# One core: the first pair's q and k on two queues by units, one mask made ahead of the branch, and the bias of the first block scaled in pieces

## The chip, the cores and the metric

The kernel runs on one core of a Trainium2 chip. The metric is the device time of one execution in microseconds (us); the kernel before has a median of 492.08 us over three runs (492.0 to 493.21).

## What is computed

The program is a banded attention, followed by two mixing layers. Cut to what matters here:

```python
scores = scale * np.matmul(q, k.transpose(0, 1, 3, 2))      # 2 batches, 8 heads, 768 rows, 64 wide
rel = pos[:, None] - pos[None, :]
is_global = pos[None, :] < int(n_global)
is_local = (rel >= 0) & (rel < int(n_local))
keep = is_global | is_local
dist = np.where(is_global & ~is_local, float(n_local), np.abs(rel))
scores = np.where(keep, scores + -slopes * dist, -1e9)
a = np.exp(scores - max); a = a / (sum + 1e-9); attn = a @ v
# then, on x = the heads side by side (2 x 768 x 512):
u = x + (relu(x.T @ w_tok1) @ w_tok2).T;  x = u + relu(u @ w_ch1) @ w_ch2
theta = x @ w_theta;  y = w_tok_r @ (x * cos(theta)) + w_tok_i @ (x * sin(theta))
u = x + y;  out = u + relu(u @ w_ch)
```

`n_global` (8) and `n_local` (96) are inputs. The program reads them at run time and branches: where they fit a band it takes the fast path (`attention_band`), else a dense one.

## The kernel before, in words

The whole kernel is written in program order (`manual_schedule`), so each engine runs its instructions in the order in which the code issues them. Around the change the order is this, with the lines of the kernel before.

**Ahead of the branch** (`run`, L895 on). SyncE (SP) issues the DMA of the two counts (`load_counts`, L237), then those of the first pair's k and q in two pieces each, k first (`load_first`, L351 and L352), and later the first pair's v and its shifted copy `a` (L367 to L370). VectorE (DVE) clears a piece of `x[1]` that serves as zeros (L907). TensorE (PE) runs ten matmuls on zeros (`warm_up`, L330). ScalarE (ACT) loads its function table and computes one exponential (L230). GpSimd (POOL) makes the identity and three integer ramps (`ramps`, L267), and ACT turns them into floats (L269). Then every engine loads the counts into registers with two TENSOR_LOADs (L913), evaluates the condition and branches (L918).

**Behind the branch** `band_bias` (L275 on) builds `base`, three 128-column blocks that are the same for all heads: `base0` (columns 0 to 128) for the first row block of each head, and `base1` (columns 128 to 384) for all others, made of `before` (96 columns), `seen` (32 columns) and `own` (128 columns). POOL makes the mask `past` (L286), the far term and `seen` (L292, L295); DVE makes the counts as floats (L290), `own` (L302, L305), `before` (L302, L305) and the first 32 columns of `base0` as a maximum of `own` and `seen` (L310); ACT copies the other 96 columns of `base0` (L308). Then each head gets a copy of all 384 columns times its slope: ACT for heads 0 and 1 (L317), POOL for heads 2 to 7 (L319).

**`attention_band`** goes through 24 units, each two row blocks of a pair of heads; a pair has three units. In step u it issues the scores of unit u (PE, L437), their bias and row minimum (DVE, L450), the exponentials (ACT, L574 and L578), the transposes of unit u-1 (PE, L484; copied back on ACT or DVE, L494 and L496) and the values of unit u-2 (PE, L406), finished on DVE and POOL (L390 to L382). Loads for the next pairs are issued inside this loop. In step 1, POOL clears two strips of the next pair's v and `a` tiles (`tiles_v`, L360), SP issues their DMAs (`load_v`, L367 to L370, which wait for those strips), then a weight job (L125), then q and k of the pair after that (L338, L339). So q and k of the third pair, which unit 6 reads first, stand in SP's queue behind v and `a` of the second pair, and these behind POOL's strips, and the strips behind POOL's six scalings of L319.

After the attention come the token mix, the channel mix and the last layer; the change does not touch them.

```python
            for u in range(N + 2):
...
                if u < N and oi + 1 < len(order) and ip == 1:
                    nx = order[oi + 1]
                    self.tiles_v(pairs_pool, pairs[nx], *nx)
                    self.load_v(pairs[nx], *nx)
                    if oi == 0:
                        self.prefetch(1)
                    if oi + 2 < len(order):
                        pairs[order[oi + 2]] = self.load_qk(pairs_pool, *order[oi + 2], bufs=2)
```

Of the kernel before, what the change touches and what calls it, by code (L numbers as in the profile page):

```python
# [15 lines left out]
F32 = mybir.dt.float32  # L16
# [3 lines left out]
AF = mybir.ActivationFunctionType  # L20
ALU = mybir.AluOpType
# [3 lines left out]
B, H, S, D = 2, 8, 768, 64  # L25
P = 128
NS = S // P
# [8 lines left out]
NG = 32  # L36
# [4 lines left out]
SCALE = 0.125  # L41
BIG = 2.56e11
# [14 lines left out]
def slope(h):  # L57
    return 2.0 ** (-(h + 1.0))
# [25 lines left out]
class Build:  # L84
# [177 lines left out]
    def ramps(self, pool):  # L262

        self.ramp = []
        for n, base, mult in ((P, 0, -1), (PREV, -PREV, -1), (NG, 0, 0)):
            ti = pool.tile([P, n], I32, name="ramp_i%d" % n)
            self.nc.gpsimd.iota(ti, pattern=[[1, n]], base=base, channel_multiplier=mult)  # L267
            tf = pool.tile([P, n], F32, name="ramp%d" % n)
            self.nc.scalar.copy(out=tf, in_=ti)  # L269
            self.ramp.append(tf)  # L270

    def band_bias(self, pool):

        nc = self.nc
        ng, nl = self.nvf[:, 0:1], self.nvf[:, 2:3]
        base = pool.tile([P, 3 * P], F32, name="base")  # L280
        base0, base1 = base[:, 0:P], base[:, P : 3 * P]
        before, seen, own = base1[:, 0:PREV], base1[:, PREV:P], base1[:, P : 2 * P]
        with self.tc.tile_pool(name="bb", bufs=1) as tp:
            d_own, d_prev, gcol = self.ramp
            past = tp.tile([P, P], F32, name="past")
            nc.gpsimd.affine_select(  # L286
                out=past, in_=d_own, pattern=[[-1, P]], compare_op=ALU.is_ge, fill=-BIG,
                base=0, channel_multiplier=1,
            )
            nc.vector.tensor_copy(out=self.nvf, in_=self.nvi)  # L290
            g = tp.tile([P, NG], F32, name="far_g")
            nc.gpsimd.tensor_scalar(  # L292
                out=g, in0=gcol, scalar1=ng, scalar2=-BIG, op0=ALU.is_ge, op1=ALU.mult
            )
            nc.gpsimd.tensor_scalar(out=seen, in0=g, scalar1=nl, scalar2=None, op0=ALU.subtract)  # L295
            nnl = tp.tile([P, 1], F32, name="nnl")
            nc.vector.tensor_scalar(out=nnl, in0=nl, scalar1=-1.0, scalar2=None, op0=ALU.mult)

            def near(out, t, dist, tag):

                far = tp.tile([P, t.shape[1]], F32, name="far" + tag)
                nc.vector.tensor_scalar(  # L302
                    out=far, in0=dist, scalar1=nnl, scalar2=-BIG, op0=ALU.is_le, op1=ALU.mult
                )
                nc.vector.tensor_tensor(out=out, in0=far, in1=t, op=ALU.add)  # L305

            near(own, past, d_own, "own")
            nc.scalar.copy(out=base0[:, NG:P], in_=own[:, NG:P])  # L308
            near(before, d_prev, d_prev, "prev")
            nc.vector.tensor_tensor(  # L310
                out=base0[:, 0:NG], in0=own[:, 0:NG], in1=seen, op=ALU.max
            )
        self.base = []
        for h in range(H):
            t = pool.tile([P, 3 * P], F32, name="base%d" % h)
            if h < 2:
                nc.scalar.activation(out=t, in_=base, func=AF.Copy, scale=slope(h) / SCALE)  # L317
            else:
                nc.gpsimd.tensor_scalar(  # L319
                    out=t, in0=base, scalar1=slope(h) / SCALE, scalar2=None, op0=ALU.mult  # L320
                )
            self.base.append((t[:, 0:P], t[:, P : 3 * P]))

# [16 lines left out]
    def load_first(self, pool):  # L342

        t = dict(
            q=pool.tile([P, S], F32, name="q_0_0", tag="q"),
            k=pool.tile([P, NS, KW], F32, name="k_0_0", tag="k"),
        )
        q, k = self.dram["q"][0, 0], self.dram["k"][0, 0]
        for i0, i1 in ((0, 2), (2, NS)):
            qs = slice(i0 * P, i1 * P)  # L350
            self.nc.sync.dma_start(out=t["k"][:, i0:i1], in_=k[:, i0:i1])  # L351
            self.nc.sync.dma_start(out=t["q"][:, qs], in_=q[:, qs])  # L352
        return t

# [1018 lines left out]
```

## Time and profile before

| | |
|---|---|
| median of three runs | 492.08 us (492.0 to 493.21) |
| the profiled execution | 493.28 us, of which the span of the core's instructions is 491.5 us |
| granted TensorE clock over the span | 1.0 of full speed |
| PE busy | 484.3 us (99%), 2836 matmuls |
| DVE, ACT, POOL busy | 317.4 us (65%), 262.9 us (53%), 180.8 us (37%) |
| chain that ended last, by engine | PE 83%, DVE 5%, ACT 5%, POOL 3%, DMA 2%, issue 1% |
| DMA | 50.66 MB, mean 103 GB/s |

The busy shares say which engine has the most work. What sets the end is read from the chain: it is followed back from the last instruction, at each step to whatever released it. The span leaves out 1.78 us of the execution's time, which lie around the instructions. In the rows below a time in the first column is counted from the span's start; "SPq", "DVEq" and the like are the sequencers that hand instructions to their engines and issue DMAs.

### The profile page before, as it was taken

Reading aid. Unit: us, or ns where it says so; the run is one execution under the profiler, and the core shown is the slowest. Engines: PE = TensorE matmul, PEld = TensorE weight load, DVE = VectorE, ACT = ScalarE, POOL = GpSimd, SP = SyncE. Lnnn points to the kernel's source line nnn. Section 1 sums busy time; section 2 is a strip of 40 time slices with the busy share of each in tenths; the row PEclk is TensorE's granted clock in tenths of the full one; section 3 lists DMA queues with packets and bytes.
Section 4 is the critical chain, followed back from the end, with each engine's and each line's share of the span. In section 5 each row is a group of like instructions: output and inputs, shape, how many; then the busy total and the mean of one; then the engine's idle time right before and its main releaser. Section 6 shows DMA issues by size and latency. Waiting matters only on the chain.

```text
span 491.5 us, 7645 instructions
## 1 busy us (share of the span) xinstructions
PE 484.3 (99%) x2836; PEld 412.3 (84%) x2836; DVE 317.4 (65%) x671; ACT 262.9 (53%) x482; POOL 180.8 (37%) x187
## 2 busy tenths in 40 slices
PE   8999999999999999999999999999999999999997
PEld 4788888787888888888888888888888889988896
DVE  4688787854776689506656564687998866351442
ACT  6888777723565554204569464646776566322010
POOL 7345534430443575401323241334554633333000
PEclk9999999999999999999999999999999999999999
DMA  6687863401454545302444222524210101000012
GB/s 194 202 261 219 280 209 119 129 2 50 134 172 107 158 137 143 94 1 85 147 133 149 87 56 60 141 87 104 68 23 22 44 22 23 21 23 22 23 71 101
DMA packets 49022, 50.66 MB, mean 103 GB/s; under 512 B 20944, under 2 KB 39888, under 8 KB 48976
## 3 DMA queue, kind: packets, MB, share of 16 engines
q1 hardware_dynamic: 48976, 50.08, 34.6%
q8 instruction: 25, 0.41, 0.3%
q14 instruction: 21, 0.17, 0.1%
HBM read 42.21 MB, written 3.15 MB: 92 GB/s over the span
## 4 chain that ended last, share of the span: by engine, by line
PE 83%; DVE 5%; ACT 5%; POOL 3%; DMA 2%; issue 1%; DVEq 0%; SPq 0%; POOLq 0%; ACTq 0%
PE gp L96 20%; PE h L96 18%; PE y L96 13%; PE v L96 7%; PE mm L96 7%; PE o L406 5%; PE th L96 5%; PE t L484 4%; PE s L437 4%; DMA k<-k 2%; POOL base L319 1%; ACT cut_xt L789 1%; DVE x L1061 1%; DVE w L1154 1%; POOL s L1180 1%
## 5 line engine op out<-in xcount | busy, mean ns | idle before, releaser
L149 POOL TENSOR_TENSOR cvt<-cvt,cvs 128x512 int32<-128x512 int32 (+1 forms) x57 | 75.1, 1318 | 177.2 <-DVE cvt L148 144.0
L96 PE MATMUL h<-wc,g 128*128 128x512 f32 x432 | 101.7, 389 | 0.0
L96 PE MATMUL gp<-xh,wc 128*128 128x512 f32 (+1 forms) x384 | 97.1, 335 | 0.0
L96 PEld LDWEIGHTS h<-wc,g 128*128 128x128 f32 x432 | 79.6, 188 | 15.2
L96 PEld LDWEIGHTS gp<-xh,wc 128*128 128x128 f32 x384 | 67.2, 189 | 8.6 <-DVE g L708 0.2
L708 DVE SCALAR_TENSOR_TENSOR g<-gp,g 128x512 fp32r<-128x512 f32 (+1 forms) x48 | 26.7, 556 | 63.4 <-ACT g L706 63.1
L96 PE MATMUL gp<-xl,wc 128*128 128x512 f32 (+1 forms) x192 | 64.3, 335 | 0.0
L96 PE MATMUL y<-wri,s 128*128 128x256 f32 (+1 forms) x288 | 52.0, 335 | 0.2 <-POOL s L1180 0.2
L96 PE MATMUL y<-wri,z 128*128 128x256 f32 (+1 forms) x288 | 51.9, 335 | 0.0
L706 ACT ACTIVATE g<-gp 128x512 fp32r<-128x512 f32 (+1 forms) x48 | 23.4, 486 | 53.2 <-PE gp L96 53.2
L96 PEld LDWEIGHTS y<-wri,s 128*128 128x128 f32 x288 | 44.7, 189 | 6.4 <-POOL s L1180 0.4
L96 PEld LDWEIGHTS y<-wri,z 128*128 128x128 f32 x288 | 44.6, 188 | 5.9
L484 PE MATMUL t<-ident,e 128*128 128x128 f32 x176 | 48.1, 285 | 0.4 <-ACT at L496 0.4
L145 DVE SCALAR_TENSOR_TENSOR cvs<-cvt,cvs 128x512 int32<-128x512 int32 (+1 forms) x57 | 44.8, 787 | 0.1
L96 PEld LDWEIGHTS gp<-xl,wc 128*128 128x128 f32 x192 | 36.0, 188 | 4.7
L450 DVE CUSTOM_DVE_ANT_0 e<-s,base 128x256 f32<-128x256 f32 (+1 forms) x96 | 32.9, 397 | 9.1 <-PE s L437 7.1
L484 PEld LDWEIGHTS t<-ident,e 128*128 128x128 f32 x176 | 31.7, 184 | 8.1 <-issue 2.3
L139 ACT ACTIVATE cvt<-raw 128x512 f32<-128x512 f32 (+1 forms) x57 | 37.2, 653 | 2.2 <-issue 2.2
L140 ACT ACTIVATE cvs<-raw 128x512 int32<-128x512 uint16 (+1 forms) x57 | 37.4, 656 | 0.0
L96 PE MATMUL th<-s,xt 128*128 128x512 f32 x144 | 34.9, 391 | 0.0
L1157 ACT ACTIVATE w<-w 128x512 f32<-128x512 f32 x12 | 7.6, 632 | 49.4 <-DVE w L1154 49.4
L406 PE MATMUL o<-v,at 128*128 128x65 f32 x192 | 32.3, 252 | 0.0
(111 smaller groups left out, 839.9 us busy)
## 6 DMA issues: line engine op xcount, KB each, us to landing
raw<-w_ch SPq DMA_DIRECT2D x28, 512.0 KB, 4.1
raw<-w_tok SPq DMA_DIRECT2D x21, 512.0 KB, 4.2
k<-k SPq DMA_DIRECT2D x7, 480.0 KB, 5.6
v<-v SPq DMA_DIRECT2D x8, 384.0 KB, 3.7
out<-o SPq DMA_DIRECT2D x11, 256.0 KB, 2.0
q<-q SPq DMA_DIRECT2D x7, 384.0 KB, 4.7
raw<-w_theta SPq DMA_DIRECT2D x4, 512.0 KB, 4.0
a<-v SPq DMA_DIRECT2D x8, 240.0 KB, 4.5
```

Source lines behind the costliest of these rows:

```text
L96: self.nc.tensor.matmul(out, lhsT=a, rhs=b, start=first and i == 0, stop=last and i == n - 1)
L139: nc.scalar.activation(out=f(t), in_=f(top), func=AF.Copy, scale=2.0**-111)
L140: nc.scalar.activation(out=s, in_=nxt, func=AF.Copy, scale=2.0**-13)
L145: nc.vector.scalar_tensor_tensor(out=s, in0=t, scalar=-(1 << 31), in1=s, op0=ALU.bitwise_and, op1=ALU.bitwise_or)
L149: nc.gpsimd.tensor_tensor(out=t, in0=t, in1=s, op=ALU.add)
L406: self.nc.tensor.matmul(po[:, j * OW : j * OW + D + 1], lhsT=at, rhs=v[:, j * (D + 1) : (j + 1) * (D + 1)], start=first, stop=last,)
L437: nc.tensor.matmul(ps[j][:, ii, c0:], lhsT=t["q"][pj, i * P : (i + 1) * P], rhs=kf[pj, i * KW - P + c0 : i * KW + P], start=True, stop=True,)
L450: nc.vector.tensor_tensor_reduce(out=e, in0=ps[j][:, ii, c0:], in1=self.base[2 * hp + j][min(i, 1)], op0=ALU.add, op1=ALU.min, scale=-SCAL ...
L484: nc.tensor.transpose(pt[:, ii, c, :], e[j][:, ii, c * P : (c + 1) * P], self.ident)
L706: nc.scalar.activation(out=hi, in_=ps, func=AF.Relu if relu else AF.Copy)
L708: nc.vector.scalar_tensor_tensor(out=lo, in0=ps, scalar=0.0, in1=f(hi), op0=ALU.max, op1=ALU.subtract)
L1157: nc.scalar.activation(out=a, in_=t, func=AF.Abs)
```

## The change

Three edits, in the first microseconds of the program.

1. `load_first`: q and k of the first pair come in three pieces each (two row blocks to a piece) rather than two. The pieces of k are issued on ACT's queue, those of q on SP's.
2. `ramps`: the floats are made by DVE rather than ACT, and POOL makes `past` right there, ahead of the branch, in a free piece of `x[1]`.
3. `band_bias`: `base0`'s first 32 columns are made ahead of `before`. ACT scales the pieces of the first block for heads 0 and 1 (96 and 32 columns each), then their 256 columns of `base1`, and copies the 96 columns into `base0` last. POOL's six scalings follow as before.

```diff
@@ -266,8 +266,13 @@
             ti = pool.tile([P, n], I32, name="ramp_i%d" % n)
             self.nc.gpsimd.iota(ti, pattern=[[1, n]], base=base, channel_multiplier=mult)
             tf = pool.tile([P, n], F32, name="ramp%d" % n)
-            self.nc.scalar.copy(out=tf, in_=ti)
+            self.nc.vector.tensor_copy(out=tf, in_=ti)
             self.ramp.append(tf)
+        self.past = self.x[1][:, 1, 0:P]
+        self.nc.gpsimd.affine_select(
+            out=self.past, in_=self.ramp[0], pattern=[[-1, P]], compare_op=ALU.is_ge, fill=-BIG,
+            base=0, channel_multiplier=1,
+        )
 
     def band_bias(self, pool):
 
@@ -282,11 +287,6 @@
         before, seen, own = base1[:, 0:PREV], base1[:, PREV:P], base1[:, P : 2 * P]
         with self.tc.tile_pool(name="bb", bufs=1) as tp:
             d_own, d_prev, gcol = self.ramp
-            past = tp.tile([P, P], F32, name="past")
-            nc.gpsimd.affine_select(
-                out=past, in_=d_own, pattern=[[-1, P]], compare_op=ALU.is_ge, fill=-BIG,
-                base=0, channel_multiplier=1,
-            )
             nc.vector.tensor_copy(out=self.nvf, in_=self.nvi)
             g = tp.tile([P, NG], F32, name="far_g")
             nc.gpsimd.tensor_scalar(
@@ -304,22 +304,29 @@
                 )
                 nc.vector.tensor_tensor(out=out, in0=far, in1=t, op=ALU.add)
 
-            near(own, past, d_own, "own")
-            nc.scalar.copy(out=base0[:, NG:P], in_=own[:, NG:P])
-            near(before, d_prev, d_prev, "prev")
+            near(own, self.past, d_own, "own")
             nc.vector.tensor_tensor(
                 out=base0[:, 0:NG], in0=own[:, 0:NG], in1=seen, op=ALU.max
             )
-        self.base = []
-        for h in range(H):
-            t = pool.tile([P, 3 * P], F32, name="base%d" % h)
-            if h < 2:
-                nc.scalar.activation(out=t, in_=base, func=AF.Copy, scale=slope(h) / SCALE)
-            else:
-                nc.gpsimd.tensor_scalar(
-                    out=t, in0=base, scalar1=slope(h) / SCALE, scalar2=None, op0=ALU.mult
-                )
-            self.base.append((t[:, 0:P], t[:, P : 3 * P]))
+            near(before, d_prev, d_prev, "prev")
+        ts = [pool.tile([P, 3 * P], F32, name="base%d" % h) for h in range(H)]
+
+        def scaled(h, src, c0, c1):
+            nc.scalar.activation(
+                out=ts[h][:, c0:c1], in_=src, func=AF.Copy, scale=slope(h) / SCALE
+            )
+
+        for h in range(2):
+            scaled(h, own[:, NG:P], NG, P)
+            scaled(h, base0[:, 0:NG], 0, NG)
+        for h in range(2):
+            scaled(h, base1, P, 3 * P)
+        nc.scalar.copy(out=base0[:, NG:P], in_=own[:, NG:P])
+        for h in range(2, H):
+            nc.gpsimd.tensor_scalar(
+                out=ts[h], in0=base, scalar1=slope(h) / SCALE, scalar2=None, op0=ALU.mult
+            )
+        self.base = [(t[:, 0:P], t[:, P : 3 * P]) for t in ts]
 
 
 
@@ -346,9 +353,9 @@
             k=pool.tile([P, NS, KW], F32, name="k_0_0", tag="k"),
         )
         q, k = self.dram["q"][0, 0], self.dram["k"][0, 0]
-        for i0, i1 in ((0, 2), (2, NS)):
-            qs = slice(i0 * P, i1 * P)
-            self.nc.sync.dma_start(out=t["k"][:, i0:i1], in_=k[:, i0:i1])
+        for i0 in range(0, NS, 2):
+            qs = slice(i0 * P, (i0 + 2) * P)
+            self.nc.scalar.dma_start(out=t["k"][:, i0 : i0 + 2], in_=k[:, i0 : i0 + 2])
             self.nc.sync.dma_start(out=t["q"][:, qs], in_=q[:, qs])
         return t
```

**ACT ahead of the branch.** `one` is the exponential of L230, the TENSOR_LOADs fetch the counts. Before:

```order
L230 ACT_TABLE_LOAD
L230 ACTIVATE one<-halfpi 128x1 [waits DVE_49]
L269 CAST ramp_130<-ramp_i_128 128x128 [waits Pool_49]
L269 CAST ramp_134<-ramp_i_132 128x96 [waits Pool_49]
L269 CAST ramp_138<-ramp_i_136 128x32 [waits Pool_49]
L913 TENSOR_LOAD nv_ptr
L913 TENSOR_LOAD nv
```

and with the change:

```order
L358 DMA k_0_102<-k 128x320 x3
L230 ACT_TABLE_LOAD
L230 ACTIVATE one<-halfpi 128x1 [waits DVE_49]
L920 TENSOR_LOAD nv_ptr
L920 TENSOR_LOAD nv
```

Three DMA issues stand ahead of the table load now, and the three conversions are gone.

**DVE ahead of the branch.** `x_66` are the zeros, a wait on Pool is one for POOL's ramps. Before:

```order
L907 MEMSET x_66 128x256
L228 MEMSET halfpi 128x1
L913 TENSOR_LOAD nv_ptr
L913 TENSOR_LOAD nv
L918 ISA
```

and with the change:

```order
L914 MEMSET x_66 128x256
L228 MEMSET halfpi 128x1
L269 CAST ramp_132<-ramp_i_130 128x128 [waits Pool_49]
L269 CAST ramp_136<-ramp_i_134 128x96 [waits Pool_49]
L269 CAST ramp_140<-ramp_i_138 128x32 [waits Pool_49]
L920 TENSOR_LOAD nv_ptr
L920 TENSOR_LOAD nv
L925 ISA
```

Three instructions that wait for POOL stand ahead of DVE's two loads now.

**ACT and POOL behind the branch.** `base_303` and the tile numbered next to it are the scaled copies of heads 0 and 1, those that POOL writes belong to heads 2 to 7. ACT before:

```order
L308 COPY base<-base 128x96 [waits DVE_49]
L317 ACTIVATE base_303<-base 128x384 [waits DVE_49,Activation_49]
L317 ACTIVATE base_305<-base 128x384
L574 ACTIVATE e_0_330<-e_0_330,mn_329 128x128 [waits DVE_49]
L574 ACTIVATE e_0_331<-e_0_331,mn_329 128x128 [waits DVE_49]
```

and with the change:

```order
L315 ACTIVATE base_303<-base 128x96 [waits DVE_49]
L315 ACTIVATE base_303<-base 128x32 [waits DVE_49]
L315 ACTIVATE base_304<-base 128x96
L315 ACTIVATE base_304<-base 128x32
L315 ACTIVATE base_303<-base 128x256 [waits DVE_49,Pool_49]
L315 ACTIVATE base_304<-base 128x256
L324 COPY base<-base 128x96
L581 ACTIVATE e_0_335<-e_0_335,mn_334 128x128 [waits DVE_49]
```

POOL before:

```order
L286 AFFINE_SELECT past<-ramp_130 128x128 [waits Activation_49]
L292 TENSOR_SCALAR far_g<-ramp_138,nvf 128x32 [waits DVE_49,Activation_49]
L295 TENSOR_SCALAR base<-far_g,nvf 128x32 [waits Pool_49]
L319 TENSOR_SCALAR base_307<-base 128x384 [waits DVE_49,Activation_49]
L319 TENSOR_SCALAR base_309<-base 128x384
```

and with the change:

```order
L292 TENSOR_SCALAR far_g<-ramp_140,nvf 128x32 [waits DVE_49]
L295 TENSOR_SCALAR base<-far_g,nvf 128x32 [waits Pool_49]
L326 TENSOR_SCALAR base_305<-base 128x384 [waits DVE_49,Activation_49,Pool_49]
L326 TENSOR_SCALAR base_306<-base 128x384
L326 TENSOR_SCALAR base_307<-base 128x384
```

ACT's copy into `base` went from the first to the last place of its bias work: two whole scalings stood behind it, six by pieces stand ahead of it. POOL's first scaling waits for that copy (Activation) as it did before; in both kernels four more scalings follow the rows shown, and then the two strips of the second pair's v and `a` (L360, now L367).

## Rows read from the trace of the kernel before

**Rows 1.** The page's first line.
```profile
span 491.5 us, 7645 instructions
```

**Rows 2.** Who PE waited for, whole span: us in total, times, longest us.
```profile
PE s L437 <- DMA q<-q: 0.8, 1, 0.8
PE s L437 <- DMA k<-k: 0.7, 1, 0.7
```

**Rows 3.** The chain that ended last, 0 to 30 us: start us, us, what.
```profile
5.99 4.59 POOL base L319 x4
...
15.81 7.91 DMA k<-k
...
23.86 0.93 PE s L437 x8
```

**Rows 4.** Instructions behind the branch: start us, us, engine, line, op, out<-in.
```profile
4.03 0.17 DVE L290 CAST nvf<-nvi 128x4 f32<-128x4 int32 x1 [2.89 <-DMA nvi<-nv]
...
4.56 0.50 POOL L292 TENSOR_SCALAR far_g<-ramp,nvf 128x32 f32<-128x32 f32 x1
4.89 0.29 DVE L305 TENSOR_TENSOR base<-farown,past 128x128 f32<-128x128 f32 x1
...
5.15 0.45 POOL L295 TENSOR_SCALAR base<-far_g,nvf 128x32 f32<-128x32 f32 x1
5.28 0.27 ACT L308 COPY base<-base 128x96 f32<-128x96 f32 x1 [2.56 <-DVE base L305]
5.39 0.26 DVE L305 TENSOR_TENSOR base<-farprev,ramp 128x96 f32<-128x96 f32 x1
5.63 0.19 DVE L310 TENSOR_TENSOR base<-base 128x32 f32<-128x32 f32 x1
...
5.92 0.94 ACT L317 ACTIVATE base<-base 128x384 f32<-128x384 f32 x2 [0.37 <-DVE base L310]
5.99 7.08 POOL L319 TENSOR_SCALAR base<-base 128x384 f32<-128x384 f32 x6 [0.39 <-DVE base L310]
...
6.80 0.81 ACT L574 ACTIVATE e<-e,mn 128x128 f32<-128x128 f32 x2
```

**Rows 5.** Instructions and DMA issues ahead of the branch, in order of time.
```profile
0.73 1.28 ACT L230 ACT_TABLE_LOAD   x1 [0.73 <-PEq L1352]
...
1.19 0.42 SPq L351 DMA_DIRECT2D k<-k  x1
...
1.26 0.50 POOL L267 IOTA ramp_i<- 128x128 int32 x3
...
1.66 0.42 SPq L352 DMA_DIRECT2D q<-q  x1
...
2.14 0.57 ACT L269 CAST ramp<-ramp_i 128x128 f32<-128x128 int32 x3
```

**Rows 6.** Register loads (L913), ACT's branch (L918): ns min/median/max, first, last start us.
```profile
L913 DVEq TENSOR_LOAD <-nv_ptr x1: 911/911/911, 0.8 to 0.8; - x1
...
L913 PEldq TENSOR_LOAD <-nv_ptr x1: 932/932/932, 1.2 to 1.2; - x1
...
L913 ACTq TENSOR_LOAD <-nv_ptr x1: 1017/1017/1017, 2.0 to 2.0; - x1
...
L913 SPq TENSOR_LOAD <-nv_ptr x1: 2880/2880/2880, 4.7 to 4.7; - x1
...
L918 ACTq COMPARE_BRANCH x2: 38/42/45, 4.7 to 115.7; - x2
```

**Rows 7.** k of the third and fourth pair: KB, us from issue to landing.
```profile
k<-k SPq DMA_DIRECT2D x1, 480.0 KB, 7.9
...
k<-k SPq DMA_DIRECT2D x1, 480.0 KB, 5.8
```

**Rows 8.** Two stretches: us, PE, PEld, DVE, ACT, POOL busy, PE clock, DMA share, GB/s.
```profile
23.16:23.86 0.70, 0.01 (x1) 0.04 (x2) 0.63 (x4) 0.70 (x3) 0.00 (x0) 1.00 0.19 60
23.86:33.74 9.88, 9.88 (x92) 8.49 (x92) 7.33 (x34) 8.10 (x20) 4.73 (x9) 1.00 0.83 267
```

## The prediction

> **What bounds the kernel now.** I read the views from the end backwards. Whole-span waits first: PE waits for data twice among its longest waits, 0.8 us for q and 0.7 us for k [rows 2], in a span of 491.5 us [rows 1]. So whatever moves the end must move PE, and the change touches only the first microseconds. The chain says which of the two waits counts. It runs from the bias work into POOL's scalings from 5.99, through SP's queue to a DMA of k issued at 15.81 that takes 7.91 us, and into PE's scores at 23.86 [rows 3]; these belong to unit 6, the first of the third pair. From there on PE is its link almost throughout: in the 9.88 us behind it PE is busy for 9.88 [rows 8]. The wait for k, 23.16 to 23.86, is therefore the place where the first part of the program sets the end. The wait for q lies ahead of it and is swallowed by it: PE, earlier by 0.8 us, would wait 0.8 us longer for k.
>
> Why is k late? It is issued behind the second pair's v, which waits for POOL's strips, and these for six scalings of 1.18 us (7.08 in all) that start at 5.99 [rows 4]. **The end hangs on when POOL starts scaling**, with no slack: PE already waits. POOL starts 0.17 us after DVE's maximum ends (5.63 + 0.19 = 5.82) [rows 4].
>
> **DVE's three conversions.** An instruction that waits for another engine holds back the register loads behind it: PE's load starts at 1.2, with its ten warm matmuls still to run, where DVE, with nothing to wait for, starts at 0.8 [rows 6]. Now three conversions stand ahead of DVE's loads, and wait for POOL's ramps, of which the third ends at 1.26 + 0.50 = 1.76 [rows 5]. DVE's loads so start at 1.8 rather than 0.8. From there to the float counts at 4.03 took 3.2 us [rows 4]; they come at 5.0. The conversions themselves (0.57 us for three on ACT [rows 5]) lie beside the loads.
>
> **`past` moved.** It leaves the branch, and far_g, which started at 4.56 behind it [rows 4], now waits for the counts, which end at 5.0 + 0.17: it starts at 5.2, and from its start to the end of `seen` is 5.15 + 0.45 - 4.56 = 1.04 us [rows 4], so 6.27. Ahead of the branch `past` waits for DVE's first conversion, and POOL's loads come some 0.7 us later; DVE's being later still hides that.
>
> **The bias on DVE.** `own` ends 4.89 + 0.29 - 4.03 = 1.15 us behind the counts' start [rows 4]: 6.15. The maximum, now ahead of `before`, needs `seen`: 6.3 to 6.5. The last step of `before` starts 0.50 behind the preceding add (4.89 to 5.39) and lasts 0.26 [rows 4]: 6.8 to 7.06. The chain that ended at 5.82 ends at 7.06.
>
> **ACT.** Three DMA issues at SP's pitch of 0.47 (1.19 to 1.66) [rows 5] push the table load from 0.73 to 2.15, by 1.4 us; the three conversions that leave ACT gave nothing, since its loads started at 2.0, as the table load ended, ahead of their execution [rows 5, 6]. ACT's first load started at 2.0 and its branch at 4.7 [rows 6]; moved by 1.4 us ACT is free at some 6.15. No row shows a DMA issue on ACT; its bounds are nothing and twice SP's 0.47 each (two sequencers at once), and I take SP's, the same instruction. Then seven operations: four pieces of 96 and 32 columns at a pitch of 0.19 (three conversions in 0.57 [rows 5]), the first at about 6.25 with `own`, the second at 6.6 with the maximum, the fourth at 7.0; the two of 256 columns with `before` at 7.16. Their pitch lies between 0.19 and the 0.42 of 384 columns (0.94 for two, 0.52 for one [rows 4]); I take 0.32, by its width nearer to the latter. The copy starts at 7.8 and takes 0.27 as at 5.28 [rows 4]: 8.07. The Trainium skill ("ScalarE: Activation LUTs", What ACT_TABLE_LOAD costs) prices a 256-column piece at 186 + 0.833 x 256 = 399 ns and takes off 93 ns of overlap, so 0.31; by it the sum would be the same within 0.02 us.
>
> **The sum.** POOL starts 0.17 behind the copy, at 8.24 in place of 5.99: **2.2 us later**, and so do the strips, v, `a`, the weight job, q and k. Six scalings and the transfers are unchanged. k's landing moves from 23.72 to 25.9 and unit 6's scores to 26.1. The exponentials of unit 0 start behind the copy, at 8.1 rather than 6.80 [rows 4]; ACT had idle time then, so half a microsecond of that reaches PE. It is covered by the wait for k, which has 2.2 us more, and would cost 0.5 us if k were not late. The split of q and k saves up to 0.8 us in unit 1, covered by the same wait. So the profiled execution of 493.28 us would become 495.5; that execution lies 1.2 us above the median of 492.08, and from the median I forecast **494.3 us**. Bounds of this case: with pitch 0.19 and the counts at 4.8, +1.7; with 0.42 and DMA issues longer by half on ACT (ACT then decides, at 6.9), +2.9: 493.8 to 495.0.
>
> **Rivals.**
> - *ACT's loads are held behind its DMA issues.* SP's first load, right behind its DMA issues, took 2.88 us, where ACT's took 1.02 [rows 6]. If ACT, now an issuer too, meets the same, it is free at 8.0; four pieces (0.76), two of 256 (0.64), the copy and the start (0.44) put POOL at 9.85: +3.9, 496.0 us. For it: the same kind of queue. Against it: ACT has 1.28 us of table load between its issues and its load, and SP's last issues were those of v and `a`, not of k. The Trainium skill ("DMA: Bandwidth & Descriptors", Queues, rings and completion order) says that SP and ACT have rings of their own on the same 16 DMA engines but no descriptor generator of their own; by it ACT could stand behind SP's v and `a` as well. No run here shows ACT as an issuer. Chance 0.16.
> - *The holding does not happen.* If DVE's loads ran ahead of the waiting conversions, the counts would come at 4.03, `seen` at 5.3, `before` at 6.1, and the copy would end at 7.1 with ACT free in time: POOL at 7.3, +1.3, 493.4 us. Rows 6 speak against it. Chance 0.10.
> - *Not slower: k's transfer gives the time back.* k took 7.9 us from its issue, the next pair's k 5.8 [rows 7]. Landing 2.1 us sooner behind its issue it would be where it was, 23.7, and the time 492.1 us; it decides from 1.5 us saved (a landing within 6.4 us). The 60 GB/s at 23.16 to 23.86 [rows 8] say that the transfer then ran at its tail, on few of the DMA engines. Against it: the five transfers ahead of it, and their order, stay. Chance 0.10.
> - *The clock falls.* PE would stand idle for up to 2.9 us rather than 0.7 ahead of unit 6. The granted clock stayed at 1.00 through the 0.7 us wait [rows 8]. If it fell to its lower level (1.2 GHz, half of 2.4), one unit's work, 9.88 / 3 = 3.3 us [rows 8], would take twice as long: 494.3 + 3.3 = 497.6 us. The Trainium skill ("TensorE: Matmul & The Clock Gate", What's actually happening) says that the clock follows how busy the PE has been; no stretch of this trace shows a fall. Chance 0.04.
>
> **How the numbers follow.** The first case has 0.60. The range leaves out the clock, half of the case in which k gives the time back, and a small part of ACT's loads being held longer: 492.4 to 496.3 us. About 0.3%, 1.5 us, is what a measurement of this kernel can tell from no change (the three runs lie 1.2 us apart). Slower by more: most of the first case, ACT's loads and the clock, 0.73. Within: the holding that does not happen, most of k's case, and the lowest end of the first, 0.22. Faster by more would need more than both of PE's waits gone, 0.8 + 0.7 us [rows 2]; 0.05 for what I do not see.
>
> **What would show it.** Right: DVE's loads start near 1.8, the counts near 5.0, ACT's table load near 2.15, POOL's first scaling near 8.2, k of the third pair is issued near 18, and PE waits two to three us for it or for the v and `a` ahead of it in the queue; the 0.8 us wait for q is gone. Wrong: POOL's first scaling below 7.5, or at 8.2 with PE waiting under 1.5 us; a load on ACT of over 2 us would mean the first rival.

## The result: slower by 1.0%, about twice the forecast

The changed kernel took 497.49 us (median of five runs, 495.9 to 500.22) against 492.98 for the kernel before (five runs): a ratio of 1.0102 over all runs (the two medians alone give 1.0091), 95% interval 1.0085 to 1.0118. The direction was as forecast. The size was not: 4.5 us instead of 2.2, and the median lies above the range, which ended at 496.3.

The profile after is of the run of 500.22 us. Its page opens with these rows:

```profile
span 498.4 us, 7652 instructions
...
PEclk9959999999999999999999999999999999999999
```

The span is 6.9 us longer than that of before [rows 1], and in the third of forty slices the granted TensorE clock fell to half. The five runs had mean clocks of 0.989, 0.997, 0.999, 0.992 and 0.996, and their times mostly follow: 500.22, 497.49, 495.9, 498.36, 496.75.

The chain still runs through the float counts, POOL's scalings, SP's queue and k of the third pair. The same instructions in the changed kernel, from the timeline (start us, us, engine, line):

```profile
6.32 0.17 DVE L290 CAST nvf<-nvi 128x4 f32<-128x4 int32 x1 [4.06 <-issue]
...
9.51 7.09 POOL L326 TENSOR_SCALAR base<-base 128x384 f32<-128x384 f32 x6 [1.83 <-DVE mn L457]
...
19.33 0.43 SPq L346 DMA_DIRECT2D k<-k  x1
...
26.64 1.65 PE L444 MATMUL s<-k,q 64*128 64x128 f32 x8 [1.99 <-DMA k<-k]
```

The counts come at 6.32 instead of 4.03 and POOL starts at 9.51 instead of 5.99 [rows 4]. PE waits 1.99 us for k, and the scores of unit 6 start at 26.64 instead of 23.86 [rows 3]. They also take 1.65 us instead of 0.93. The stretches table says why (us, PE, PEld, DVE, ACT, POOL busy, PE clock, DMA share, GB/s):

```profile
24.65:26.64 1.99, 0.00 (x2) 0.03 (x1) 0.60 (x2) 1.37 (x3) 1.13 (x2) 0.93 0.94 315
26.64:36.56 9.92, 9.92 (x50) 8.32 (x51) 4.47 (x21) 3.86 (x9) 2.40 (x3) 0.50 0.73 235
36.56:41.09 4.53, 4.53 (x44) 3.92 (x42) 2.71 (x12) 3.36 (x9) 1.23 (x4) 1.00 0.00 0
```

For 9.92 us behind the wait PE worked at half its clock: 50 matmuls, where 9.88 us of before held 92 [rows 8]. Unit 9's scores start 14.38 us behind unit 6's (26.64 to 41.02) instead of 9.81 (23.86 to 33.67). So the profiled run lost 2.8 us up to unit 6 and 4.6 us to the clock behind it, and got back some 0.5 later.

Why the counts are so late stands in the register loads (line 920; ns min/median/max, first and last start us):

```profile
L920 PEldq TENSOR_LOAD <-nv_ptr x1: 1013/1013/1013, 1.2 to 1.2; - x1
...
L920 DVEq TENSOR_LOAD <-nv_ptr x1: 1531/1531/1531, 1.9 to 1.9; - x1
L920 ACTq TENSOR_LOAD <-nv_ptr x1: 1669/1669/1669, 2.2 to 2.2; - x1
L920 PEldq TENSOR_LOAD <-nv x1: 2774/2774/2774, 2.3 to 2.3; - x1
...
L920 DVEq TENSOR_LOAD <-nv x1: 1961/1961/1961, 3.4 to 3.4; - x1
```

In the kernel before the second loads of DVE and PE were these:

```profile
L913 DVEq TENSOR_LOAD <-nv x1: 1346/1346/1346, 1.8 to 1.8; - x1
...
L913 PEldq TENSOR_LOAD <-nv x1: 1084/1084/1084, 2.2 to 2.2; - x1
```

DVE's first load starts at 1.9, close to the forecast 1.8, and then both its loads are long: 1.53 and 1.96 us, where they took 0.91 [rows 6] and 1.35 before. PE's second load starts when it did before, within 0.1 us, and takes 2.77 us instead of 1.08; that engine's program did not change, so something around it did. The DMAs of that time are late too (KB, us from issue to landing; k's first piece and the counts):

```profile
k<-k ACTq DMA_DIRECT2D x1, 160.0 KB, 4.0
nvi<-nv SPq DMA_DIRECT2D x1, 2.0 KB, 3.8
```

In the kernel before each of the two needed 2.8 us:

```profile
k<-k SPq DMA_DIRECT2D x1, 160.0 KB, 2.8
...
nvi<-nv SPq DMA_DIRECT2D x1, 2.0 KB, 2.8
```

### The profile page after: what moved, and what is told of

The parts are those of the page before. It is cut to its first block, busy times and chain, and to the rows that moved or that the text cites. A ratio compares the mean times of both kernels' runs of the same rounds, so it can differ in the third digit from the quotient of the medians.

```text
span 498.4 us, 7652 instructions
## 1 busy us (share of the span) xinstructions
PE 490.2 (98%) x2836; PEld 416.1 (83%) x2836; DVE 318.4 (64%) x674; ACT 262.8 (53%) x483; POOL 180.7 (36%) x187
## 4 chain that ended last, share of the span: by engine, by line
PE 83%; DVE 5%; ACT 5%; POOL 3%; DMA 1%; issue 1%; DVEq 1%; SPq 0%; POOLq 0%; ACTq 0%
PE gp L96 20%; PE h L96 18%; PE y L96 13%; PE v L96 7%; PE mm L96 7%; PE o L413 6%; PE th L96 4%; PE t L491 4%; PE s L444 4%; DMA k<-k 1%; POOL base L326 1%; ACT cut_xt L796 1%; DVE x L1068 1%; DVE w L1161 1%; DVEq L920 1%
## 5 line engine op out<-in xcount | busy, mean ns | idle before, releaser
L491 PE MATMUL t<-ident,e 128*128 128x128 f32 x176 | 50.0, 295 | 0.8 <-ACT at L503 0.4
L491 PEld LDWEIGHTS t<-ident,e 128*128 128x128 f32 x176 | 33.0, 192 | 9.8 <-issue 4.2
```

Source lines behind the costliest of these rows:

```text
L491: nc.tensor.transpose(pt[:, ii, c, :], e[j][:, ii, c * P : (c + 1) * P], self.ident)
```

## The experiments

Two theories were on record when the first four ran: that two queues which issue at once slow the start, loads and transfers alike, and that the loads crowd each other because edit 2 moves them together. The second question was whether the clock falls because PE idles.

**Edit 1 alone, on the kernel before.**

```diff
-        for i0, i1 in ((0, 2), (2, NS)):
-            self.nc.sync.dma_start(out=t["k"][:, i0:i1], in_=k[:, i0:i1])
+        for i0 in range(0, NS, 2):
+            self.nc.scalar.dma_start(out=t["k"][:, i0 : i0 + 2], in_=k[:, i0 : i0 + 2])
```

> The kernel before with edit 1 alone (k on ACT's queue, three pieces each). Theory 'two queues': two queues that issue at once slow the first microseconds for transfers and for the register loads alike. It expects DVE's two loads to take 1.5 + 2.0 us as in the changed kernel instead of 0.9 + 1.35, the counts at 5.2 instead of 4.03 us, POOL's first scaling at about 7.2 instead of 5.99, PE's wait for k at 1.5 to 2 us, and the time 1.2 us above before. Rival 'crowding': the loads are slow because edit 2 moves DVE's and POOL's loads together with ACT's. It expects DVE's loads at 0.9 + 1.35 here, POOL at 5.99 within 0.2, and the time of before within 0.4 us.

494.09 us against 492.85: 1.0032 (1.0019 to 1.0046). Its loads and POOL's start:

```profile
L913 DVEq TENSOR_LOAD <-nv x1: 2365/2365/2365, 1.8 to 1.8; - x1
...
L913 PEldq TENSOR_LOAD <-nv x1: 2401/2401/2401, 2.6 to 2.6; - x1
```

```profile
7.65 7.08 POOL L319 TENSOR_SCALAR base<-base 128x384 f32<-128x384 f32 x6 [0.39 <-DVE base L310]
```

Without edits 2 and 3 the loads are about as long as in the changed kernel: DVE's two take 0.92 + 2.37 = 3.29 us, against 1.53 + 1.96 = 3.49 there and 2.26 before. The counts come at 5.06 and PE waits 1.6 us for k. Crowding by edit 2 falls. The clock fell in the profiled run here as well, and not at once (from the wait's start at 23.59 us):

```profile
23.59:25.19 1.60, 0.00 (x1) 0.03 (x1) 0.79 (x4) 1.60 (x4) 0.57 (x2) 1.00 0.69 222
25.19:30.06 4.87, 4.87 (x32) 4.47 (x32) 2.24 (x10) 2.29 (x7) 1.83 (x2) 0.65 1.03 280
```

In the first microsecond behind the wait the clock was still 0.96; from 26.2 us on it was 0.50.

**Edits 2 and 3 alone: k and q back on SP in two pieces.**

```diff
-        for i0 in range(0, NS, 2):
-            self.nc.scalar.dma_start(out=t["k"][:, i0 : i0 + 2], in_=k[:, i0 : i0 + 2])
+        for i0, i1 in ((0, 2), (2, NS)):
+            self.nc.sync.dma_start(out=t["k"][:, i0:i1], in_=k[:, i0:i1])
```

> The changed kernel with edit 1 undone (k and q on SP's queue, two pieces each). Theory 'two queues' expects the register loads at their old length (DVE 0.9 + 1.35), the counts at 5.0, POOL's first scaling at 8.0 to 8.3, k of the third pair 2 to 2.3 us later than before, and 2.2 us above before, plus what the clock loses if it falls in the wait. Rival 'crowding' expects DVE's loads at 1.5 + 2.0, the counts at 6.3, POOL at 9.5 and the time of the changed kernel, some 4.5 us above before.

494.92 us, 1.0043 (1.0026 to 1.006), at clocks from 0.993 to 1.0. From its timeline and its register loads:

```profile
5.18 0.17 DVE L290 CAST nvf<-nvi 128x4 f32<-128x4 int32 x1 [2.92 <-issue]
...
8.38 7.08 POOL L326 TENSOR_SCALAR base<-base 128x384 f32<-128x384 f32 x6 [1.83 <-DVE mn L457]
```

```profile
L920 DVEq TENSOR_LOAD <-nv_ptr x1: 1500/1500/1500, 1.9 to 1.9; - x1
...
L920 DVEq TENSOR_LOAD <-nv x1: 852/852/852, 3.4 to 3.4; - x1
```

This is nearly the sum of the prediction: counts at 5.0, POOL at 8.24, 2.2 us (2.1 measured). DVE's first load took 1.50 us here and its second 0.85, 2.35 together, near the 2.26 of before. Two of its five runs lost clock all the same (498.08 us at 0.993, the profiled one, and 495.58 at 0.996), so the 2.1 us are those of the median.

**All six pieces on SP's queue.**

```diff
-            self.nc.scalar.dma_start(out=t["k"][:, i0 : i0 + 2], in_=k[:, i0 : i0 + 2])
+            self.nc.sync.dma_start(out=t["k"][:, i0 : i0 + 2], in_=k[:, i0 : i0 + 2])
```

> The changed kernel with all six pieces on SP's queue (k ahead of q). If two queues slow the start, this one is as fast as the run with edit 1 undone: the counts at 5.0, POOL at 8.0 to 8.3, 2 to 3 us above before. If the smaller pieces do it, the counts stay at 6.3, POOL at 9.5, 4.5 us above before. ACT's table load starts at 0.73 in either case.

495.07 us, 1.0061 (1.0035 to 1.0087); the counts at 4.79, POOL at 7.99. The smaller pieces are not at fault, the use of the second queue is. (With it the six transfers are also issued sooner, the last at about 2.1 us instead of 3.55; the runs do not separate the two.) Its profiled run of 494.55 us also had PE wait 1.92 us, as long as the changed kernel's, and kept its clock:

```profile
23.40:25.32 1.92, 0.01 (x1) 0.03 (x1) 0.80 (x4) 1.81 (x4) 0.88 (x2) 1.00 0.79 245
25.32:35.20 9.88, 9.88 (x92) 8.50 (x92) 7.17 (x33) 6.98 (x17) 3.84 (x8) 1.00 0.72 231
```

Others of its runs did not: 0.990 at 499.42 us, 0.996 at 496.48 and 496.36, 0.997 at 495.24.

**PE's wait filled with matmuls on zeros.**

```diff
+                    if u == 6:
+                        self.warm_up(6)
                     exps = scores(u)
```

> The changed kernel with six matmuls on zeros put ahead of the scores of unit 6, where PE waits 2.0 us for k; nothing else moves. Theory 'clock': the clock falls because PE idles there, and that costs the runs between 0.5 and 4.5 us. It expects a granted clock of 1.00 in every stretch, PE's scores of unit 6 still at 26.6 us and all runs within 1 us of 495.8 us, the changed kernel's run at a clock of 0.999. Rival 'the wait alone': the clock has another cause; it expects the clock at 0.99 to 0.997 again and a median of 497.5 us.

`warm_up(6)` issues six matmuls on zeros. 495.83 us (495.45 to 497.08, four runs), clocks of 1.0 three times and 0.999. The stretches:

```profile
24.65:26.43 1.78, 0.96 (x4) 0.26 (x4) 0.49 (x2) 1.49 (x3) 1.08 (x2) 1.00 0.86 282
26.43:36.31 9.88, 9.88 (x92) 8.50 (x92) 7.17 (x33) 6.98 (x17) 3.65 (x8) 1.00 0.77 239
```

POOL is as late (9.62), k nearly as late, PE still waits for it (0.82 us behind the zeros), and the clock stays. That takes 1.7 us off the changed kernel's median, with no other change. One run of four (497.08) lies outside the expected 1 us, without a fall of the clock that would explain it.

**The copy first again**, on the run with edit 1 undone.

```diff
             near(own, self.past, d_own, "own")
+            nc.scalar.copy(out=base0[:, NG:P], in_=own[:, NG:P])
...
-        nc.scalar.copy(out=base0[:, NG:P], in_=own[:, NG:P])
```

> The run with edit 1 undone, and ACT's copy of 96 columns put back into the first place of its bias work. If the copy's last place costs POOL what the sum says (ACT's six scalings ahead of it, about 1.0 us), POOL's first scaling starts at about 7.3 instead of 8.4 and the time falls to 1.0 to 1.3 us above before, mostly at a clock of 1.00. If POOL is late only by the counts, it stays at 8.2 or later and 2 us above before.

```profile
5.46 0.17 DVE L290 CAST nvf<-nvi 128x4 f32<-128x4 int32 x1 [3.29 <-issue]
...
7.72 7.09 POOL L326 TENSOR_SCALAR base<-base 128x384 f32<-128x384 f32 x6 [0.89 <-ACT base L316]
```

From the counts to POOL's start it is 2.26 us here, 3.20 in the run with edit 1 undone and 3.19 in the changed kernel: the copy's last place costs 0.94. The counts came 0.3 later than in the run with edit 1 undone, so POOL gained only 0.66. Nothing ahead of the counts differs between these two programs, so 0.3 us is what the loads vary by, with one queue (PE's second took 1.62 us here and 1.03 there). In time this is a miss: 494.64 us, 1.0046 (1.0022 to 1.0071), not clearly below the 494.92, and 2.1 us above the before measured beside it, as there. Its eight runs go from 493.27 to 498.85, the slowest at a clock of 0.988; three of them lie at 493.3 to 493.6, about where the expectation put it.

**The strips ahead of the scalings**, in both kernels. `rest` holds POOL's scalings of heads 2 to 7, which leave `band_bias`.

```diff
             pairs[order[1]] = self.load_qk(pairs_pool, *order[1], bufs=2)
+            self.tiles_v(pairs_pool, pairs[order[1]], *order[1])
+            self.rest()
             for u in range(N + 2):
...
-                    self.tiles_v(pairs_pool, pairs[nx], *nx)
+                    if oi:
+                        self.tiles_v(pairs_pool, pairs[nx], *nx)
```

The changed kernel with this move:

> The changed kernel with the two strips of the second pair's v and a made by POOL ahead of its six scalings, so that the DMAs of v, a, the weight job, q and k no longer wait for these. If the whole loss runs through that queue (k's landing, and the clock that falls in the wait for it), PE does not wait for k at unit 6, the clock stays at 1.00 and the time is that of before within 1 us (492 to 494), though the register loads are as slow as in the changed kernel. If the slow start costs PE something of its own (its first scores came 1.2 us later, the exponentials of unit 0 2.5 us later), that shows now: 494 to 495.

493.43 us, 1.0018 (1.0009 to 1.0027), ten runs from 493.19 to 493.86, all at 0.999 or 1.0. Counts at 6.47 and POOL at 9.67, later than ever, and yet PE waits for no k:

```profile
PE s L447 <- issue: 0.5, 1, 0.5
PE t L494 <- ACT e L586: 0.4, 1, 0.4
PE t L494 <- ACT e L590: 0.3, 1, 0.3
```

So most of the loss came through that one queue, by k's landing and by the clock behind it: 4.1 us between the two medians, 3.6 when each is counted against the before measured beside it. The rest, 0.9 us, is PE's own later start: the scores of units 0 and 2 start at 6.12 and 11.34 us here, and at 5.26 and 9.71 in the kernel before with the same move, the next run.

The kernel before with the move, and with q and k in six pieces on SP besides:

> The kernel before with the same move of the two strips. The sum expects PE's wait of 0.7 us for k gone and 0.5 to 0.8 us less time than before, 492.1 against 492.85. If k still lands late for another reason (the first pairs' transfers crowd each other when they start sooner), the wait stays and so does the time.

> The same, and the first pair's q and k in six pieces on SP's queue. PE's wait of 0.8 us for q at unit 1 should go too, and now nothing behind it swallows it: 0.3 to 0.8 us less than the run with the strips alone. If ACT's exponentials bound units 0 to 2 anyway, the time is that of the run with the strips alone, within 0.3 us.

Both missed: 492.52 us, 0.9999 (0.999 to 1.0008), and 492.43 us, 0.9999 (0.999 to 1.0008). The wait for k is gone in both profiles, and the time is that of before. Two more traces of the kernel before were taken to see what the gain had been counted against.

> The kernel before, unchanged, for a second trace of it. In nine traces so far the time from unit 6's first score to the end of the span, at a clock of 0.999 to 1.00, is 467.2 to 467.7 us. So a run at before's median of 492.6 (span 490.8) should have unit 6's scores at 23.2 to 23.6 and a wait for k of 0 to 0.5 us instead of 0.7: that would be why moving the strips gains nothing. If the wait is 0.7 or more at a time of 492.6, the gain went somewhere else.

> The same once more: unit 6's scores at the span minus 467.2 to 467.7 us, and the wait for k longer the longer the span.

492.3 and 492.71 us. The first has its unit 6 here, and neither trace has a wait for k at all:

```profile
23.09 0.93 PE L437 MATMUL s<-k,q 64*128 64x128 f32 x8
```

```profile
k<-k SPq DMA_DIRECT2D x1, 480.0 KB, 6.8
```

In the second unit 6 starts at 23.34, and k landed 7.2 us behind its issue. The 0.7 us of the profile that the prediction read [rows 2] belong to a run of 493.28 us in which k took 7.9 [rows 7]; in the other two it landed 0.4 to 0.5 us ahead of unit 6. The issue of that DMA alone took 1.55 us in the first profile, and 0.43 in each of the other two, which may be why (the second row is of the first further trace):

```profile
15.81 1.55 SPq L339 DMA_DIRECT2D k<-k  x1
```

```profile
15.76 0.43 SPq L339 DMA_DIRECT2D k<-k  x1
```

In all ten traces with a mean clock of 0.999 or 1.0 from unit 6's first score to the end of the span it is 467.1 to 467.7 us. The start of unit 6 and the clock behind it are all that the first part of the program passes on.

**When do two queues hurt?** The last two put k's three issues on ACT behind its table load (`load_first_k`), and only k's first piece on ACT.

```diff
                     self.constants(cp)
+                    self.load_first_k(first)
```

> The changed kernel with k's three issues on ACT behind its table load, so from about 2.1 us instead of 0.74. What slows the first microseconds could be two queues that start at the same moment (0.74 to 2.1 us), or any time in which both issue. The first expects the counts at 5.0 to 5.3 and POOL at 8.2 to 8.5; the second the counts at 6 or later again. Either way k of unit 0 lands later than in the changed kernel if a transfer needs as long as there (4.0 us from its issue): PE's first scores at about 6.2 or later.

```diff
-            self.nc.scalar.dma_start(out=t["k"][:, i0 : i0 + 2], in_=k[:, i0 : i0 + 2])
+            eng = self.nc.scalar if i0 == 0 else self.nc.sync
+            eng.dma_start(out=t["k"][:, i0 : i0 + 2], in_=k[:, i0 : i0 + 2])
```

> The changed kernel with k's first piece alone on ACT's queue, the other five pieces on SP's. If a second queue in use is enough to slow the start, the first transfers take 3.8 to 4.0 us again and the counts come at 6.0 to 6.4. If it is the number of transfers in two queues at once, the counts come at 4.8 to 5.3 as with one queue. ACT's table load moves by 0.47 us only, to 1.2.

Behind the table load: 497.64 us, 1.0102 (1.0085 to 1.0118), the counts at 6.72. With one piece: 493.99 us, 1.0049 (1.0024 to 1.0074), the counts at 4.73, POOL at 7.92, as with one queue; k's piece on ACT landed after 3.3 us. So a second queue in use is not enough: with three transfers on each the start is slow, with one on ACT it is not. Two on ACT were not tried. From the timeline of the run behind the table load:

```profile
0.73 1.28 ACT L230 ACT_TABLE_LOAD   x1 [0.73 <-PEq L1364]
1.20 0.87 ACTq L364 DMA_DIRECT2D k<-k  x2
...
2.10 0.45 ACTq L364 DMA_DIRECT2D k<-k  x1
```

The first two issues start at 1.20, in the middle of the table load, so "behind" it is 0.46 us later than in the changed kernel and not 1.4, and the moment of the start was put to the test more weakly than meant: a shift of 0.46 us changes nothing, a longer one was not tried. Its PE scores of unit 0 came at 5.57, not at 6.2 or later. The counts' own transfer landed after 2.9 us here, almost as before, and the counts came later than in any other run: it is the register loads that hold them (DVE's took 1.87 and 2.03 us). ACT's first load, right behind its last issue, took 3.06 us. What in the chip makes loads and transfers slow then was not found.

## Why the prediction was wrong

**Right.** The bound (POOL's start, through SP's queue, to k of the third pair), the direction, the holding of DVE's loads behind its conversions (1.8 forecast, 1.9 measured), the 3.2 us from the counts to POOL's start (8.24 - 5.0; measured 3.19), and that the wait for q goes without a gain. Of the signs that the prediction named, ACT's table load at 2.15 and PE's wait of two us (1.99) are there; k is issued at 19.33, not near 18. With edit 1 undone the sum holds as it stands: POOL at 8.38, 2.1 us. That the time agrees so closely is partly luck, since the sum had no slack and two traces of before have 0.4 to 0.5 us.

**The first step that failed: "From there to the float counts at 4.03 took 3.2 us; they come at 5.0".** It kept the length of DVE's loads. They took 3.49 us instead of 2.26, and the counts came at 6.32. This is a term of 1.3 us, and edit 1 brings it: DVE's two loads take 3.29 us with edit 1 alone, and 2.35 with edits 2 and 3 alone. The prediction had a rival for slow loads and tied it to ACT alone, as a follower of its own DMA issues, because SP's load behind such issues was the only long one in the rows [rows 6]. ACT's first load did take 1.67 us (it started at 2.2, straight behind the issues: the table load that was held against this rival lay beside it, not between), but PE's and POOL's, which issue no DMA, grew as well, and DVE's decided. That the rival's start for POOL, 9.85, lies near the measured 9.51 is luck. The page cited there ("DMA: Bandwidth & Descriptors" of the Trainium skill) says in its section Issuing engines are not separate DMA queues that issuing from several engines only saves the time of the issue. The saving is there: SP issues v at 2.60 us, with all six pieces on SP at 4.03. The runs add a price that the page does not have: with k's three pieces on ACT, its first landed 4.0 us behind its issue instead of 2.8, the counts 3.8 instead of 2.8.

**The second: the clock, at a chance of 0.04.** "The granted clock stayed at 1.00 through the 0.7 us wait" was true, and it was taken as evidence for a wait of up to four times that length, 2.9 us, of which no row spoke. In the changed kernel four runs of five had a mean clock below 0.999; the profiled run gave up 4.6 us, the rival had priced 3.3. That its 497.6 us lies so near the median is luck: by the estimate below the median run lost more ahead of unit 6 and less to the clock than the rival has it. This step puts the median outside the range: without the fall, in the filled wait, it is 495.83 us, which lies inside. The filled wait shows the cause: PE's idling. The rule of the Trainium skill ("TensorE: Matmul & The Clock Gate", What's actually happening), that the clock follows how busy PE has been, agrees: 0.50 for 9.92 us behind the wait, 1.00 with matmuls in it. But the wait's length does not settle it by itself: 1.92 us passed without a fall in one run, and 1.60 us did not in another (edit 1 alone, 0.65 from 25.19 to 30.06).

**A smaller one: "with no slack: PE already waits".** The profiled run of before had an unusual transfer of k; in two others PE did not wait for it. This made the forecast gain of the moved strips, 0.5 to 0.8 us, nothing. In the changed kernel k needed 7.17 us from its issue, so its landing moved by less than POOL's start did, 2.8 against 3.5 us.

**And one that cost nothing.** ACT's first load, at 2.0 before, was held by its conversions and not by the table load: without them it starts at 1.2, under the table load (the run with edit 1 undone). ACT was free in time all the same.

For the median of 4.5 us an estimate, since that run has no trace: unit 6 later by some 3.4 us (26.64 against 23.09 and 23.34 in the two further traces of before), and the rest the clock. The filled wait, which has the first without the second, is 3.0 us above before.

## What to carry to other kernels

A wait of the tensor engine has a second price, its clock: a delay of 2 us ahead of a long run of matmuls cost up to 4.6 us more, differently from run to run. A few matmuls on zeros took that away, but moving the work that the queue waits for (here two small strips) took the wait away. Before a load goes to a second queue, look at what else reads memory in those microseconds: here the program's own register loads grew, on PE, which the edit does not touch, from 1.1 to 2.8 us. And a wait of 0.7 us in one profile may be that run's alone; two more traces cost little.

## What the runs showed of the hardware

Register loads on PE, POOL, DVE and ACT were slower when SP and ACT each had issued three transfers of 128 to 160 KB (PE's second 2.77 us, against 1.08), and PE's second was not when ACT had issued one (1.13). With SP's queue alone it varied from 1.03 to 1.62. SP's own first load was not slower (1.30 us, against 2.88). ACT issues DMAs while its table load runs (issue at 1.20, table load 0.73 to 2.01), but a table load behind DMA issues waits for them (2.15 in the changed kernel). Three issues on ACT took 1.38 us, SP's three 1.36. Behind the wait for k the granted clock was 0.50 over 9.92 us in the changed kernel; its mean was 0.52 over 5.89 us with edits 2 and 3 alone and 0.65 over 4.87 us with edit 1 alone, each with PE busy throughout. In the last of these it fell only after PE had worked for about a microsecond again.
